# Beacon attention and a max-out FFN on one core: the first batch in token halves, loads reordered behind it

## The chip, the cores and the metric

The kernel runs on one core of a Trainium2 chip. The metric is the device time of one execution in microseconds; each time given for a kernel is a median of several executions. The profile is of one further execution and counts from its first instruction to its last (its span).

## The reference

Eight batches (B), eight heads (H), 576 tokens (S), head width 64 (D), 16 beacon keys and values ahead of the tokens. What is computed, cut to the core:

```
k_all, v_all = concat([beacon_k, k]), concat([beacon_v, v])      # 592 keys
scores = q @ k_all.T / 8 ; beacons seen by all, tokens causal
x = softmax(scores) @ v_all            -> (4608 tokens, 512)
h = max(x @ w1, x @ w2, x @ w3)        # 512 -> 768
out = h @ w_out                        # 768 -> 512, float32
```

Inputs and output are float32; the kernel multiplies in bf16.

## The kernel before

**Work.** Heads go in pairs: 4 pairs a batch, 32 pairs in all, and two pairs (a quad) share one product with the values. For a pair `p` the kernel loads q and k, casts them to bf16 (`cast_pair`, on POOL, L192), turns them so that the head width lies on the partitions (`turn`, `turn_apart`, `turn_pair`: transposes on TensorE, copies out of PSUM by DVE or ACT), and from batch 4 on has the DMA turn them by way of a copy in DRAM. `emit_scores` (L375) writes the transposed scores of one of four key-tile groups into a PSUM tile `sc` (two of them) and lets ACT exponentiate it into `at_sb`. `emit_masks` (L400) zeroes what lies past the diagonal, on POOL (an affine select, L410) or, for the first pairs, on DVE (a product with a triangle, L408). `emit_pv` (L430) makes, for one half of the tokens of a quad, the sums of the exponentials (weights of ones) and the products with the values; `finish_pv` (L462) inverts the sums on ACT (Ln, then Exp) and multiplies on DVE into `xT`, the FFN's input.

**FFN units.** Nine blocks of 512 tokens, each with 18 units `mm1_unit` (one weight matrix, 128 of 768 columns: 4 matmuls of 512 columns, then a copy or a running maximum on DVE) and 4 units `mm2_unit` (6 matmuls, a copy, a store). They stand in one list; `emit_ffn` (L543) takes the next one if a limit `allowed` permits and if the batches that it needs are finished (`ready`). They are what TensorE does between the pieces of attention.

**Order.** The program order on each engine is written out by hand. `start` and the table `fine_at` (L641) order pairs 0 to 4 in four steps a pair, with dummy matmuls (`keep_busy`) between them; later pairs have two steps (score groups 0 and 1; groups 2 and 3), and from pair 5 on `allowed` spreads 20 units over nine steps and then 22 units over each batch. The table `plan` hangs loads and casts on steps.

**Loads.** SP's queue carries q, k, v and the beacons, in the order of the list `loads` (L567); a cast through `C` (L580) is followed by the next load. Staging buffers `st`: 9. The FFN's weights are loaded and cast by POOL's own DMA queue (`load_w` L235, `load_w_out` L242): w1 at pair 2, w2 at the end of pair 3, w3 at pair 5, `w_out` at pair 6. POOL issues these in program order with its casts and masks. The values come in two pieces a batch (three and two key tiles), with one 256-byte run per token and head.

Of the kernel before, what the change touches and what calls it, by code (L numbers as in the profile page):

```python
# [16 lines left out]
def kernel(  # L17
# [29 lines left out]
    QR = 6  # L47
    QP = S // QR
    PR = 9
    PP = S // PR  # L50
    P_NINE = 4
# [18 lines left out]
    groups = [  # L70
# [5 lines left out]
    NG = len(groups)  # L76
    g_width = [sum(q1 - q0 for _, q0, q1 in pieces) for pieces in groups]
    g_base = [2 * sum(g_width[:gi]) for gi in range(NG)]
    AT_W = 2 * sum(g_width)
    assert max(g_width) <= 512  # L80
# [9 lines left out]
    st_pool = ctx.enter_context(tc.tile_pool(name="st", bufs=9))  # L90
    pair_pool = ctx.enter_context(tc.tile_pool(name="pair", bufs=3))
    v_pool = ctx.enter_context(tc.tile_pool(name="v", bufs=2))
# [25 lines left out]
    make_identity(nc, ident)  # L118
# [7 lines left out]
    for i in range(NT):  # L126
        z = const.tile([128, NKP], BF16, name=f"kT{i}")
        nc.vector.memset(z[:, NK:NKP], 0.0)
        kTs.append(z)
    nc.vector.memset(ones, 1.0)  # L130
    tri = const.tile([128, 128], BF16, name="tri")
    nc.gpsimd.memset(tri, 1.0)
    nc.gpsimd.affine_select(
        out=tri,
        in_=tri,
        compare_op=ALU.is_ge,
        fill=0.0,
        base=0,
        pattern=[[1, 128]],
        channel_multiplier=-1,  # L140
    )
# [19 lines left out]
    def load_pair(p, k_queue=None):  # L161
        b, g, j0 = place(p)
        hs = slice(head(g, j0), head(g, j0) + 2)
        st = new_stage(("pair", p))
        for i, (src, queue) in enumerate(((q, nc.sync), (k, k_queue or nc.sync))):
            if p < P_NINE:
                queue.dma_start(
                    out=st[:, i * PR * D : (i + 1) * PR * D],
                    in_=src[b, hs].rearrange("h (p r) d -> (h p) (r d)", r=PR),
                )  # L170
            else:
                queue.dma_start(  # L172
                    out=st[0:QP, i * NQ2 : (i + 1) * NQ2].rearrange("p (h x) -> p h x", h=2),
                    in_=src[b, hs].rearrange("h (p r) d -> p h (r d)", r=QR),
                )

    def cast_piece(p, i, cast):
        st = stage["pair", p]
        if p < P_NINE:
            t16 = pair_pool.tile([128, PR, D], BF16, name=f"t16{i}")  # L180
            cast(
                t16.rearrange("x r d -> x (r d)"), st[:, i * PR * D : (i + 1) * PR * D]
            )
        else:
            t16 = pair_pool.tile([QP, QR, 2, D], BF16, name=f"p16{i}")
            cast(  # L186
                t16.rearrange("p r h d -> p h r d"),
                st[0:QP, i * NQ2 : (i + 1) * NQ2].rearrange("p (h r d) -> p h r d", h=2, r=QR),
            )
        stage["pair16", p, i] = t16  # L190
# [26 lines left out]
    def cast_v(b, piece, cast):  # L217
# [6 lines left out]
        while t < t_hi:  # L224
            t1 = t + 1
            while b > 0 and t1 < t_hi and k_rows[t1] == k_rows[t]:
                t1 += 1
            n = k_rows[t]
            cast(  # L229
                v_sb[0:n, t:t1].rearrange("p t h d -> p (t h d)"),  # L230
                st[0:n, (t - t_lo) * H * D : (t1 - t_lo) * H * D],
            )
            t = t1

# [19 lines left out]
    def turn_beacons(b0, b1, src):  # L254
        n = Nb * (b1 - b0)
        ps = ffn_psum.tile([128, PPB, n], BF16, name="fps")
# [40 lines left out]
    def turn(p, i, ps):  # L297
        src = stage.pop(("pair16", p, i))
        if p >= P_NINE:
            for r in range(QR):  # L300
                nc.tensor.transpose(
                    ps[:, r * QP : (r + 1) * QP],
                    src[:, r].rearrange("p h d -> p (h d)"),
                    ident[0:QP, 0:QP],
                )
            return
        for r in range(PR):
            for e in range(2):
                hs = slice(64 * e, 64 * e + 64)
                nc.tensor.transpose(  # L310
                    ps[hs, r * PP : (r + 1) * PP],
                    src[hs, r],
                    ident[hs, hs],
                    tile_position=(64 * e, 64 * e),
                )

    def rows(p):
        return PR if p < P_NINE else QR

    def evac_q(p, ps, copy):  # L320
        copy(
            qTs[p % NT].rearrange("d (p r) -> d p r", r=rows(p)),
            ps.rearrange("d (r p) -> d p r", r=rows(p)),
        )
# [5 lines left out]
    def evac_k(p, ps, copy):  # L330
        kT = kTs[p % NT]
        copy(  # L332
            kT[:, Nb:NK].rearrange("d (p r) -> d p r", r=rows(p)),
            ps.rearrange("d (r p) -> d p r", r=rows(p)),
# [9 lines left out]
    def turn_pair(p, q_copy):  # L344
        banks = [pv_bank(i, [128, 1024], BF16) for i in range(2)]
        for i in range(2):
            turn(p, i, banks[i][:, 0:S])
        evac_q(p, banks[0][:, 0:S], q_copy)
        evac_k(p, banks[1][:, 0:S], by_dve)
# [12 lines left out]
    def at_view(p, t, e, q0, q1):  # L362
        for gi, pieces in enumerate(groups):
            off = g_base[gi] + e * g_width[gi]
            for t_, lo, hi in pieces:
                if t_ == t and lo <= q0 and q1 <= hi:
                    return at[p][0 : k_rows[t], off + q0 - lo : off + q1 - lo]
# [3 lines left out]
    def both_heads(p, gi):  # L371
        W = g_width[gi]
        return at[p][:, g_base[gi] : g_base[gi] + 2 * W].rearrange("k (e c) -> k e c", e=2)

    def emit_scores(p, gi):  # L375
# [6 lines left out]
        for t, q0, q1 in groups[gi]:  # L382
# [12 lines left out]
            out=both_heads(p, gi), in_=ps[:, :, 0 : g_width[gi]], func=AF.Exp, scale=scale  # L395
        )

    def emit_masks(p, gi, dve=False):
        off = 0
        for t, q0, q1 in groups[gi]:  # L400
            n = k_rows[t]
# [28 lines left out]
    def emit_pv(quad, hf, first=0, last=len(passes), apart=False):  # L430
        b, g = divmod(quad, n_quad)
        v_sb = v_tiles[b]
        if first == 0:
# [6 lines left out]
        for part, bank, lo, ca, cb in passes[first:last]:  # L440
            qa, qb = hf * HALF + ca, hf * HALF + cb
            ts = [t for t in range(n_kt) if q_min[t] < qb]
            for t in ts:
                q0 = max(qa, q_min[t])
                for j in range(4):
                    lhsT = (
                        ones[0 : k_rows[t]]
                        if part == 0
                        else v_sb[0 : k_rows[t], t, head(g, j), part - 1 : D : 2]
# [12 lines left out]
    def finish_pv():  # L462
# [3 lines left out]
        b, g = divmod(quad, n_quad)  # L466
# [5 lines left out]
        c0 = b % RING * S + hf * HALF  # L472
        for part, bank, lo, ca, cb in passes[1:]:
# [5 lines left out]
        if g == n_quad - 1 and hf == 1:  # L479
            ready[0] = b  # L480
# [3 lines left out]
    hTs = {}  # L484

    alone = [False]

    def mm1_unit(tb, ft, i, pool, name):
        if ft == 0 and i == 0:
            hTs[tb] = ffn_h.tile([128, n_ft, TOKB], BF16, name="hT")  # L490
        hT = hTs[tb]
# [12 lines left out]
        if i == 0:  # L504
            (by_act if alone[0] else by_dve)(hT[:, ft, :], ps)  # L505
        else:
            nc.vector.tensor_max(hT[:, ft, :], hT[:, ft, :], ps)  # L507
# [23 lines left out]

    units = []
    for tb in range(n_tokb):
        last_b = (TOKB * (tb + 1) - 1) // S
        for i in range(3):
            for ft in range(n_ft):
                units.append((last_b, mm1_unit, (tb, ft, i)))
        for tt in range(TOKB // 128):
            units.append((last_b, mm2_unit, (tb, tt)))
    UPB = len(units) // n_tokb  # L540
    done = [0]

    def emit_ffn(limit, pool=None, name="fps"):  # L543
        if done[0] + 1 <= limit and done[0] < len(units) and units[done[0]][0] <= ready[0]:
            _, fn, args = units[done[0]]
# [21 lines left out]
    loads = [L(load_pair, 0, nc.scalar), L(load_pair, 1, nc.scalar)] + load_pairs(2, 4)  # L567
    loads += [L(load_v, 0, 0), L(load_beacons, 1, B_PE, bk32_1), L(load_v, 0, 1)]
    loads += load_pairs(4, 7) + load_v_pieces(1) + load_pairs(7, 8)
# [17 lines left out]
    def start():  # L587
        keep_busy(15)
        next_load()
        load_beacons(0, 1, bk32_0, nc.scalar)  # L590
        next_load(10)
        cast_piece(0, 0, by_dve)
        cast_piece(0, 1, by_act)
        stage.pop(("pair", 0))
        by_pool(bk16_0, bk32_0)
        next_load()
        q_ps = ffn_psum.tile([128, S], BF16, name="fps")
        k_ps = ffn_psum.tile([128, S], BF16, name="fps")
        turn(0, 0, q_ps)
        turn(0, 1, k_ps)  # L600
        evac_q(0, q_ps, by_act)
        evac_k(0, k_ps, by_dve)
        turn_beacons(0, 1, bk16_0)
        keep_busy(4)
        C(cast_pair, 1, by_pool, by_pool)()
# [5 lines left out]


    P_FINE = PPB + 1

    def steps(p):
        return [[gi] for gi in range(NG)] if p < P_FINE else [[0, 1], [2, 3]]

    at_step(0, 0, C(cast_pair, 2, by_pool, by_pool))
    at_step(0, 1, C(cast_pair, 3, by_pool, by_pool))
    at_step(1, 0, *[L(emit_masks, 0, gi) for gi in range(NG)])  # L620
    at_step(1, 0, C(cast_v, 0, 0, by_pool))
    at_step(1, 1, C(cast_v, 0, 1, by_pool))
    at_step(1, 2, L(by_pool, bk16_1, bk32_1))
    at_step(1, 3, C(cast_pair, 4, by_pool, by_pool))
    at_step(2, 0, L(load_w, 0, 0, d_ff))
    at_step(2, 2, C(cast_pair, 5, by_pool, by_pool))
    at_step(3, 2, C(cast_pair, 6, by_pool, by_pool))
    at_step(3, 3, L(load_w, 1, 0, d_ff))
    at_step(4, 1, C(cast_v, 1, 0, by_pool))
    at_step(4, 2, C(cast_v, 1, 1, by_pool))  # L630
    at_step(5, 0, L(load_w, 2, 0, d_ff))
    at_step(5, 0, C(cast_pair, 7, by_pool, by_pool))
# [126 lines left out]
```

The softmax here doesn't subtract the row's maximum and nothing guards it: scores larger than these inputs give would overflow.

## Time and profile before

| | |
|---|---|
| median of 5 runs | 303.93 us (301.91 to 304.79) |
| profiled execution | 304.35 us |
| its span | 302.6 us |
| TensorE busy | 283.9 us, 94% of the span |
| DVE, ACT, POOL busy | 175.4, 143.2, 128.6 us |
| granted TensorE clock, mean | 0.982 |
| read from HBM, written | 35.13 MB, 14.22 MB |

In the profile a line such as `L497 PE MATMUL fps<-xT,w_sb` is a group of instructions of one source line; PE is TensorE, PEld its weight loads, DVE is VectorE, ACT ScalarE, POOL GpSimd, SPq the queue of SyncE that only issues DMAs. "Idle before" is time in which the engine did nothing ahead of an instruction, and the name behind the arrow is what ended it. In the tables of windows, PEclk is the granted TensorE clock (1.00 is full speed) and the DMA share is the mean busy share of 16 DMA engines; a mean above 1 comes from packets that overlap on an engine.

### The profile page before, as it was taken

What the parts mean: (1) busy time and instruction counts of PE and PEld (TensorE: products, weight loads), DVE (VectorE), ACT (ScalarE), POOL (GpSimd) and SP (SyncE); (2) the same over time, 40 slices, a digit from 0 to 9 for tenths busy, and PEclk for the clock granted to TensorE, in tenths of its full rate; (3) what the DMA queues carried; (4) which work ended last, traced back from release to release, by engine and by line L of the source; (5) the groups of instructions that cost most, each with busy time, mean ns of one, the idle gap of its engine ahead of it and who ended that gap; (6) DMA issues with size and microseconds to landing.
All of it is one profiled execution on the core that took longest, in us unless ns stands there. A gap on an engine that the chain in (4) does not pass through costs nothing.

```text
span 302.6 us, 8591 instructions
## 1 busy us (share of the span) xinstructions
PE 283.9 (94%) x3532; PEld 148.0 (49%) x3563; DVE 175.4 (58%) x330; ACT 143.2 (47%) x220; POOL 128.6 (42%) x261
## 2 busy tenths in 40 slices
PE   7796869999999999999999999999999999999995
PEld 4454234554455545454545687645454544444442
DVE  2968335656667466646564657365746575275373
ACT  3786554574555364635463556455545531400300
POOL 3876194455667684465446644562243210000000
PEclk9979797999999999999999999999999999999999
DMA  7999999999799889989998998466402001102003
GB/s 259 208 246 216 214 261 232 215 241 219 174 315 203 220 251 247 192 202 264 281 187 197 258 260 144 114 171 154 101 36 106 2 2 69 72 0 110 30 2 139
DMA packets 83095, 51.55 MB, mean 170 GB/s; under 512 B 62064, under 2 KB 76656, under 8 KB 83056
## 3 DMA queue, kind: packets, MB, share of 16 engines
q1 hardware_dynamic: 80976, 47.23, 66.8%
q0 software_dynamic: 1648, 3.15, 5.5%
q8 instruction: 28, 0.46, 0.7%
q10 hardware_dynamic: 432, 0.62, 0.7%
q14 instruction: 11, 0.09, 0.1%
HBM read 35.13 MB, written 14.22 MB: 163 GB/s over the span
## 4 chain that ended last, share of the span: by engine, by line
PE 80%; DMA 9%; SPq 3%; DVE 3%; POOL 2%; issue 2%; ACT 0%; DVEq 0%
PE fps L497 40%; PE fps L514 13%; PE pv L451 11%; PE sc L385 8%; PE sc L497 5%; DMA st<-in_v_dram 4%; DMA st<-in_k_dram 3%; PE sc L514 2%; DMA st<-in_q_dram 2%; SPq L249 1%; SPq L213 1%; POOL p L186 1%; DVE kT L332 1%; DVE hT L507 1%; SPq L172 1%
## 5 line engine op out<-in xcount | busy, mean ns | idle before, releaser
L394 ACT ACTIVATE at_sb<-sc 128x992 bf16<-128x992 f32 (+3 forms) x128 | 103.6, 862 | 100.8 <-PE sc L385 100.8
L497 PE MATMUL fps<-xT,w_sb 128*128 128x512 bf16 (+1 forms) x627 | 139.8, 360 | 3.1 <-issue 1.2
L497 PEld LDWEIGHTS <-w_sb 128*128 128x128 bf16 x720 | 66.1, 98 | 72.7 <-issue 17.3
L410 POOL TENSOR_SCALAR_AFFINE_SELECT at_sb<-at_sb 128x256 bf16<-128x256 bf16 (+2 forms) x145 | 52.7, 384 | 99.2 <-ACT at_sb L394 97.7
L507 DVE TENSOR_TENSOR hT<-hT,fps 128x512 bf16<-128x512 bf16 x96 | 65.8, 686 | 45.2 <-PE fps L497 45.1
L186 POOL CAST p<-st 96x768 bf16<-96x768 f32 x56 | 44.7, 823 | 1.6 <-DMA st<-in_q_dram 0.9
L514 PE MATMUL fps<-w_out_sb,hT 128*128 128x512 bf16 x173 | 40.6, 379 | 0.9 <-issue 0.8
L505 DVE CAST hT<-fps 128x512 bf16<-128x512 f32 x42 | 29.0, 690 | 21.5 <-PE fps L497 21.4
L385 PE MATMUL sc<-qT,kT 64*128 64x288 bf16 (+4 forms) x384 | 36.4, 288 | 3.0 <-ACT at_sb L394 1.2
L522 DVE COPY y<-fps 128x512 f32<-128x512 f32 x30 | 20.7, 689 | 27.9 <-PE fps L514 27.3
L514 PEld LDWEIGHTS <-hT 128*128 128x128 bf16 x216 | 20.5, 98 | 25.0 <-DVE hT L507 1.3
L474 DVE TENSOR_TENSOR xT<-pv,recip 128x288 bf16<-128x288 f32 (+2 forms) x93 | 27.2, 348 | 3.8 <-ACT recip L471 2.2
L451 PE MATMUL pv<-at_sb,v_sb 128*32 128x192 bf16 (+4 forms) x1352 | 28.6, 230 | 0.1
L385 PEld LDWEIGHTS <-kT 64*128 64x128 bf16 x384 | 13.8, 94 | 28.9 <-issue 19.8
L451 PEld LDWEIGHTS <-v_sb 128*32 128x32 bf16 (+1 forms) x1408 | 24.6, 97 | 3.3 <-issue 2.1
L229 POOL CAST v_sb<-st 128x512 bf16<-128x512 f32 (+2 forms) x26 | 21.5, 841 | 10.4 <-DMA st<-in_v_dram 10.3
L451 PE MATMUL pv<-at_sb,ones 128*32 128x288 bf16 (+4 forms) x492 | 17.6, 258 | 2.2 <-POOL at_sb L410 2.1
L497 PE MATMUL sc<-xT,w_sb 128*128 128x512 bf16 x71 | 18.3, 379 | 0.1
L469 ACT ACTIVATE lnd<-pv 128x288 f32<-128x288 f32 x31 | 12.9, 416 | 7.8 <-PE pv L451 7.8
L451 PEld LDWEIGHTS <-ones 128*32 128x32 bf16 (+1 forms) x512 | 11.0, 96 | 9.5 <-issue 7.8
L507 DVE TENSOR_TENSOR hT<-hT,sc 128x512 bf16<-128x512 bf16 x12 | 8.2, 688 | 12.5 <-PE sc L497 6.8
L505 ACT CAST hT<-sc 128x512 bf16<-128x512 f32 x6 | 3.5, 585 | 23.7 <-PE sc L497 23.7
(47 smaller groups left out, 115.5 us busy)
## 6 DMA issues: line engine op xcount, KB each, us to landing
st<-in_q_dram SPq DMA_DIRECT2D x32, 288.0 KB, 5.1
out_dram<-y SPq DMA_DIRECT2D x36, 256.0 KB, 2.4
st<-in_k_dram SPq DMA_DIRECT2D x30, 288.0 KB, 5.5
st<-in_v_dram SPq DMA_DIRECT2D x24, 256.0 KB, 6.1
w_sb<-in_moe_w_dram POOLq DMA_DIRECT2D x6, 384.0 KB, 9.4
q_dram<-p SPq DMA_DIRECT2D x16, 144.0 KB, 2.4
k_dram<-p SPq DMA_DIRECT2D x16, 144.0 KB, 2.4
st<-in_v_dram SPq DMA_DIRECT2D x8, 224.0 KB, 6.0
```

The lines of the kernel that those rows point to most:

```text
L186: cast(t16.rearrange("p r h d -> p h r d"), st[0:QP, i * NQ2 : (i + 1) * NQ2].rearrange("p (h r d) -> p h r d", h=2, r=QR),)
L229: cast(v_sb[0:n, t:t1].rearrange("p t h d -> p (t h d)"), st[0:n, (t - t_lo) * H * D : (t1 - t_lo) * H * D],)
L385: nc.tensor.matmul(ps[:, e, off : off + q1 - q0], kT[hs, 128 * t : 128 * t + 128], qT[hs, q0:q1], start=True, stop=True, tile_position=(64 ...
L394: nc.scalar.activation(out=both_heads(p, gi), in_=ps[:, :, 0 : g_width[gi]], func=AF.Exp, scale=scale)
L410: nc.gpsimd.affine_select(out=view, in_=view, compare_op=ALU.is_ge, fill=0.0, base=x0, pattern=[[0, 2], [1, hi - lo]], channel_multiplier=-1,)
L451: nc.tensor.matmul(ps[bank][32 * j : 32 * j + 32, lo + q0 - qa : lo + qb - qa], lhsT, at_view(PPQ * quad + j // 2, t, j % 2, q0, qb), star ...
L474: nc.vector.tensor_mul(xT[:, 2 * g + part - 1, c0 + ca : c0 + cb], ps[bank][:, lo : lo + cb - ca], recip[:, ca:cb],)
L497: nc.tensor.matmul(ps[:, o0 : o0 + n], w_in[i][:, ct, 128 * ft : 128 * (ft + 1)], xT[:, ct, x0 : x0 + n], start=(ct == 0), stop=(ct == n_c ...
L505: (by_act if alone[0] else by_dve)(hT[:, ft, :], ps)
L507: nc.vector.tensor_max(hT[:, ft, :], hT[:, ft, :], ps)
L514: nc.tensor.matmul(ps, hT[:, ft, 128 * tt : 128 * (tt + 1)], w_out_sb[:, ft, :], start=(ft == 0), stop=(ft == n_ft - 1),)
L522: nc.vector.tensor_copy(y, ps)
```

## The change

It rewrites the first batch and what feeds it, and moves some work in the later pairs. Lines here are of the file before unless the diff is meant.

- **Batch 0 in token halves.** q and k of pairs 0 to 3 are loaded as halves of 288 tokens on 96 partitions. The first halves of pairs 0 and 1 come by SP and ACT and are cast by DVE and ACT. All others come as six POOL transfers (`load_quad`: four heads of q or k, cast by the DMA), issued before anything else on POOL but two small masks. The score groups of batch 0 are cut so that group 0 holds all that the first 288 queries need; masks of the first halves go to DVE. A hand-written list `first_steps` replaces `fine_at`: group 0 of pairs 0 to 3 first, turns two pairs ahead, then the other groups. Eight dummy matmuls of the middle go, 12 + 2 instead of 15 + 4 stay at the start.
- **Loads.** Values of batch 0 come right behind the first two halves on SP. w1 is requested behind the cast of the third value tile, w2 behind that of the fifth, w3 behind the cast of pair 4, `w_out` in pair 5. The loads of pairs 4 and 5 wait for a one-column DVE memset of their buffer, which stands late in the first steps; all later SP loads stand behind them. Eight `st` buffers instead of nine.
- **First FFN block in halves.** Its units for w1 and w2 become 12 units of 256 tokens and two column tiles each (8 matmuls of 256 columns); the first six need only the first token halves. Six run within the first steps, the other 16 of the block are spread over 11 steps from pair 4 on.
- **Later pairs.** The turn of the next pair moves from the second step to the first and from the `pv` banks to an `sc` tile (pairs 7 to 15); its k is copied out before its q; the beacons' columns are copied by DVE instead of POOL. ACT inverts the sums right behind `emit_pv`, DVE multiplies at the end of the step. Some units use an `sc` tile.

```diff
+    groups_0 = [
+        [(0, 0, HALF), (1, q_min[1], HALF), (2, q_min[2], HALF)],
+        [(0, HALF, S), (3, q_min[3], S)],
+        [(1, HALF, S), (4, q_min[4], S)],
+        [(2, HALF, S)],
+    ]
...
+        if gate:
+            gate.memset(st[0:QP, 0:1], 0.0)
...
+    def load_quad(g, h):
+        for i in range(2):
+            t16 = const.tile([QP, 4, HR, D], BF16, name=f"quad{g}{h}{i}")
+            nc.gpsimd.dma_start(
+                out=t16.rearrange("p h r d -> p h (r d)"), in_=half_source(g, h, i, 0, 4)
+            )
...
-    def turn_pair(p, q_copy):
-        banks = [pv_bank(i, [128, 1024], BF16) for i in range(2)]
+    def turn_pair(p, q_copy, shared=True):
+        if shared:
+            ps = sc_psum.tile([128, 2, 1024], BF16, name="sc")
+            banks = [ps[:, i, 0:S] for i in range(2)]
...
-    loads = [L(load_pair, 0, nc.scalar), L(load_pair, 1, nc.scalar)] + load_pairs(2, 4)
-    loads += [L(load_v, 0, 0), L(load_beacons, 1, B_PE, bk32_1), L(load_v, 0, 1)]
-    loads += load_pairs(4, 7) + load_v_pieces(1) + load_pairs(7, 8)
+    loads = [L(load_v, 0, 0), L(load_v, 0, 1), L(load_beacons, 1, B_PE, bk32_1)]
+    loads += load_pairs(6, 7) + load_v_pieces(1) + load_pairs(7, 8)
...
+        load_quad(1, 0)
+        load_quad(0, 1)
+        load_quad(1, 1)
+        next_load(3)
...
+    first_steps = [
+        ((0, 0), [T(2, 0, False)]),
+        ((1, 0), [M(0, 0, True), T(3, 0, True), V(0), V(1)]),
+        ((2, 0), [T(0, 1, False), V(2), L(load_w, 0, 0, d_ff)]),
+        ((3, 0), [T(1, 1, True), M(1, 0, True), M(2, 0, True)]),
+        ((0, 1), [M(0, 1)]),
+        ((0, 2), [T(2, 1, False), M(3, 0, True), M(0, 2), V(3), V(4)]),
+        ((0, 3), [M(0, 3, True), L(load_w, 1, 0, d_ff)]),
+        ((1, 1), [P(0, 0), M(1, 1)]),
+        ((1, 2), [T(3, 1, False), finish_pv, M(1, 2)]),
+        ((1, 3), [P(1, 0, True), M(1, 3, True)]),
+        ((2, 1), [finish_pv, G(4), cast_p]),
+        ((2, 2), [M(2, 1), M(2, 2, True)]),
+        ((2, 3), [P(0, 1, False, 0, 2), F(1), M(2, 3)]),
+        ((3, 1), [P(0, 1, False, 2, 4), M(3, 1, True), G(5), F(1), L(turn_beacons, 1, B_PE, bk16_1)]),
+        ((3, 2), [F(1), finish_pv, next_7, M(3, 2)]),
+        ((3, 3), [F(2), M(3, 3), L(cast_pair, 4, by_pool, by_pool), L(load_w, 2, 0, d_ff), P(1, 1),
+                  L(turn_apart, 4, 0), L(turn_apart, 4, 1), finish_pv, F(1), L(cast_pair, 5, by_pool, by_pool)]),
+    ]
+    at_step(4, 0, C(cast_pair, 6, by_pool, by_pool))
+    at_step(5, 0, C(cast_v, 1, 0, by_pool))
+    at_step(5, 0, L(load_w_out))
+    at_step(5, 1, C(cast_v, 1, 1, by_pool))
+    at_step(5, 1, C(cast_pair, 7, by_pool, by_pool))
...
+        if tb == 0:
+            for n, lo in ((0, 0), (need, MID)):
+                for i in range(2):
+                    for ft in range(0, n_ft, 2):
+                        units.append((n, mm1_halves, (tb, ft, i, lo, lo + MID)))
...
-                    if n_step <= 9:
-                        allowed = 2 + n_step * (UPB - 2) / 9
+                if n_step <= N_FIRST:
+                    allowed = first + n_step * (UPB - first) / N_FIRST
```

In `first_steps`, T turns a half, M masks, P is `emit_pv`, V casts a value tile, G is a gated pair load and F runs FFN units. `N_FIRST` is 11, and `first` is 6.

## The prediction

> **What bounds the kernel now.** I read the busy time by stage first, because the page's totals (TensorE 94%) mix stages. Columns: busy us and count for PE, PEld, DVE, ACT, POOL, then granted clock, DMA share, GB/s. I cut where pair 4's scores, pair 5's, pair 9's and the tail begin.
>
> ```profile
> 0.00:25.00 25.00, 19.47 (x359) 11.33 (x359) 15.91 (x36) 17.18 (x26) 15.88 (x33) 0.93 0.99 235
> 25.00:35.40 10.40, 7.76 (x151) 4.08 (x152) 5.35 (x16) 4.86 (x9) 2.90 (x6) 0.85 1.14 222
> 35.40:66.30 30.90, 27.04 (x330) 13.09 (x334) 16.69 (x30) 17.64 (x26) 18.60 (x40) 0.94 1.10 232
> 66.30:250.00 183.70, 181.20 (x2433) 97.33 (x2458) 110.68 (x209) 95.65 (x146) 91.20 (x183) 1.00 0.78 180
> 250.00:302.60 52.60, 48.46 (x271) 22.13 (x268) 26.73 (x41) 7.87 (x14) 0.00 (x0) 0.99 0.16 61
> ```
>
> From 66.3 us on TensorE is the bound, with 2.5 us idle in 184; only more work or new stalls count there. Before 66.3 no engine is full, the clock sags, and the DMA share is 1. The chain of waits, followed back from 60 us, says that the DMA orders this stage:
>
> ```profile
> 16.46 8.76 DMA st<-in_k_dram
> 25.28 0.83 POOL p L186
> ...
> 26.22 13.05 DMA st<-in_v_dram
> 39.32 0.61 POOL v_sb L229
> ...
> 42.42 1.59 POOL p L186 x2
> 44.01 0.72 POOL at_sb L410 x2
> 44.77 0.65 PE pv L451 x33
> ```
>
> Batch 1's last values take from 26.2 to 39.3 us; then POOL casts pair 7 before it masks what TensorE waits for. TensorE's timeline shows what such waits cost twice:
>
> ```profile
> 32.75 2.76 PE L497 MATMUL fps<-xT,w_sb 128*128 128x512 bf16 x6 [0.22 <-issue]
> ...
> 44.42 0.55 PE L451 MATMUL pv<-at_sb,ones 128*32 128x176 bf16 x6 [2.11 <-POOL at_sb L410]
> ...
> 45.58 2.87 PE L497 MATMUL fps<-xT,w_sb 128*128 128x512 bf16 x7 [0.16 <-issue]
> ```
>
> Behind a lull, matmuls stand 0.43 us apart; unhindered ones 0.216. The value loads are late because of who shares the DMA (queues, 26 to 34 us, then 38 to 46 us: packets, MB, share of 16 engines):
>
> ```profile
> q0 software_dynamic: 513, 1.43, 90.6%
> q1 hardware_dynamic: 1134, 0.29, 19.3%
> ```
> ```profile
> q1 hardware_dynamic: 1476, 2.09, 108.5%
> ```
>
> Weights (POOL's queue) take the engines; 256-byte value packets get little.
>
> **What the skill says.** "DMA: Bandwidth & Descriptors", section Queues, rings and completion order: an engine takes queues in turn, a packet each; so weights win time by packet size. The 90.6 against 19.3% agree. "TensorE: Matmul & The Clock Gate", Part 1: idle TensorE falls to half its clock, in windows of 3413 ns; the trace's 0.43 against 0.216 us agrees. "GPSIMD Engine Reference", section Key points: POOL shares its SBUF interfaces with DVE instructions that have two SBUF inputs or use a two-port mode. The same beacon copy agrees (min/median/max ns):
>
> ```profile
> L328 POOL COPY kT<-bT x10: 186/193/194, 41.2 to 111.2; 128x16 bf16<-128x16 bf16 x10
> L328 DVE COPY kT<-bT x5: 155/550/2166, 9.5 to 27.7; 128x16 bf16<-128x16 bf16 x5
> ```
>
> **Where to compare.** Before, 19 FFN units are done when pair 9's scores start (66.3 us); after the change 6+16x10/11 = 20. The extra one is an `mm2` unit, 6x0.216 = 1.3 us. So the mark to beat is 67.6 us. From there both run the same units (22 by the next step, 22 a batch).
>
> **The DMA sum.** Prices: an `mm1` weight 4.0 us (q0: 0.906x8 us for 1.43 MB written; one weight is 0.79 MB); a pair of 0.59 MB on 96 partitions 2.25 us (2.09 MB in 8 us); a batch of values, 1.18 MB in 256-byte packets, 5.8 us (the queues of 57.8 to 60.3 us give 204 GB/s); the four beacon loads about 0.6. First packets move at 2 us. No row shows the six quad transfers (1.77 MB read in 768-byte runs, written as 384 bytes). Below: 5.2 us at `w_out`'s read rate (queues of 52 to 57 us: 0.70 MB written, twice that read, in 0.819x5 us, 342 GB/s). Above: 13.5, if they go at half the 96-partition rate. I take that rate, 262 GB/s: 6.8.
>
> After, in the order of need: start 2.0, first halves 2.25, quads 6.8, values 5.8, beacons 0.6 = 17.4. Then w1 and w2 8.0, pairs 4 to 6 6.8, w3 4.0, batch 1's values 5.8, pair 7 2.25 = 44.3. `w_out` is requested when three tiles of batch 1's values are cast (about 43) and takes turns with pair 7: +2. Lane waits idle the DMA a little (before: share 0.64 in 12 to 15 us, 1.1 lost): +1. Pair 7 lands at about 47. Before it landed at about 41, but w3 and `w_out` only afterwards, and three of its first pairs went at 400 GB/s on 128 partitions.
>
> **TensorE from pair 7 on.** The changed order turns pair 7 in pair 6's first step, and TensorE is in order: all behind it waits. POOL casts its k (0.82): 47.8; 12 transposes 0.5: 48.3. Rest of pair 6: two units of 4x0.216 = 0.86, scores 0.5, gaps 0.2: 50.5. Pair 7: scores 1.06, products 1.61, turn 0.5, three units 2.6, gaps 0.2 = 6.0: 56.5. Pair 8: 1.06+0.79+0.5+0.86+two `mm2` 2.6+0.2 = 6.0: 62.5. Pairs 8 and 9 land 2.25 us apart behind pair 7 plus the rest of `w_out`, ahead of their turns at about 53 and 59. **Gain 67.6-62.5 = 5.1 us.**
>
> **Is TensorE there by then?** First steps, per engine: ACT 16 exponentials 13, inversions 4x0.85, small ones 1.5 = 17.9; DVE 16 half copies of 0.40 (half of 0.75), masks 3.5, FFN copies 6x0.69, xT 4x0.88, casts and pair 4's copies 3.5 = 21. From 4.2 us on that is 25 at least. The values come 1:1 with quad packets, so their third tile lands near 16; its cast frees w1's request (before at 20.7) and the first value products. The fifth tile then shares with w1, so w2 is asked for near 21. That pushes my walk along TensorE's order to pair 4's scores at about 34. Pairs 4 and 5 (4 us each: scores 1.06, turn 0.5, 2 to 3 units) end at 42: ahead of pair 7's 47. So the first steps have 4 us of cover; beyond that they cost one for one. The gates cost nothing: they hold pair 4 back to about 23, while w1 and w2 fill the engines; pair 4 then lands near 29, its cast ends by 31.
>
> **The rest.** Eight dummy matmuls (0.33 each) go: they filled waits, so nothing; cover gone, a half-clock window of 3.4 us costs up to 1.7. Before had three by 66.3 us; I expect as many (0, range -1.7 to +1.7). The turn a step earlier, k first: turned batches take 32.8 and 31.6 us against 30.5 unturned; 12 transposes a pair explain 2.0 and 1.5, so at most 0.3 in the one, nothing in the other. An `sc` tile taken by a turn makes group 3 wait for q's copy (ACT 0.65), hidden by a unit. Beacon copies on DVE: 0.15 if POOL is quiet, 2.17 at worst; DVE is 60% busy and TensorE has two `fps` banks (1.7 us) ahead, so 0 to 0.5 each for 11 pairs. Later inversion order, DVE products at the step's end, `sc` for units: the batches without turns show 0.2 us idle in 30.5, so nothing to win. I take 0 for all.
>
> 302.6-5.1 = 297.5 of span; with the 1.7 us around it 299.3. The profiled execution is 0.4 above the median: 298.9, say **299**.
>
> **Rivals.**
> A, the above: the DMA paces pairs 5 to 7, gain 3 to 7. Chance 0.50; 297 to 301.
> B, TensorE-bound refill: if weights overlap better with value packets (shares add up to 1.1), pair 7 is on time and TensorE runs through: 34 + 12 `mm1` 10.4 + two `mm2` 2.6 + five pairs at 3.0 less two value products 2.4 = 59.6, gain 8: 296, down to 293. Against it: before, the same engines were full up to 66 us. Chance 0.20.
> C, it does not do what it says: the weights' requests sit behind value casts on POOL in order, so they come no sooner; `w_out` ahead of pair 7 and a cold clock use up the rest. Gain 0 to 2: 302 to 304. Chance 0.13.
> D, slower: the quads. All turns of six of eight halves hang on them. At 13.5 us instead of 6.8 everything behind, the weights too, is 7 us late: 306. From 8 us more (15 us; over 100 ns for each of the 144 packets an engine) it is slower than 307. For it: small written packets, POOL's descriptor queue beside busy DVE; against: 1024-byte packets of `w_out` do well. With the beacon copies stalling as well, 308. Chance 0.17.
>
> **Numbers.** Likeliest A, 299, its own range 296 to 302. Leaving out D and the edge of B gives 293 to 306. About 1% (3 us) is what a measurement of this kernel tells from no change. Faster than 300.9: A 0.42, B 0.20, C 0.03 = 0.65; within: A 0.08, C 0.10 = 0.18; slower 0.17.
>
> **What would show it.** Right: quads landed by 15 to 16 us; pair 4's scores at 31 to 35; the chain before 60 us still DMA into POOL casts; TensorE waiting at pair 7's transposes till about 48; pair 9's scores at about 62; batches from pair 9 on 30.5 to 32.8 as before. Wrong: first turns waiting for quads beyond 18 us; DVE's beacon copies near 2 us in pairs 6 to 15; batches longer by 0.5 us.

## The result, and the profile after

The change brought nothing: 304.38 us median (302.69 to 308.42, 41 runs) against 303.25 (301.48 to 306.08, 78 runs), ratio 1.0043, 95% interval 1.003 to 1.0057, so slower by some 0.4%. Forecast was 299. Ratios here leave out single slow executions and come near the ratio of the means, so they differ from the ratio of the listed medians by up to 0.002. The profiled execution took 303.93 us, its span 302.2; the one before had 304.35 and 302.6. Profiles of single executions thus differ by 1.5 us from what the medians say, and nothing below rests on less than that unless several profiles agree.

Times by stage, columns as before, cut at pair 4's, pair 9's scores and the tail (first line: up to 25 us):

```profile
0.00:25.00 25.00, 20.20 (x280) 11.09 (x284) 12.30 (x51) 14.10 (x22) 12.61 (x29) 0.65 1.02 174
25.00:37.20 12.20, 11.61 (x214) 8.25 (x207) 6.71 (x18) 4.76 (x10) 5.13 (x9) 0.87 0.76 177
37.20:66.60 29.40, 25.88 (x368) 15.16 (x372) 18.31 (x36) 21.23 (x31) 18.03 (x37) 1.00 1.14 235
66.60:250.00 183.40, 180.53 (x2475) 97.62 (x2498) 113.43 (x214) 96.60 (x147) 91.60 (x179) 1.00 0.87 186
250.00:302.20 52.20, 47.35 (x215) 21.24 (x218) 26.20 (x40) 7.57 (x14) 0.00 (x0) 0.99 0.16 61
```

Pair 4's scores come at 37.2 us (before 25), pair 9's at 66.5, where the forecast had 62.5 and the mark to beat was 67.6. So 1.1 us was won by then. Behind it the step from pair 12's first exponential to pair 13's is 0.4 us longer (8.51 against 8.13) and the stretch behind pair 31 0.6 longer; 0.3 is won between. What is new is in the first two rows: a clock of 0.65 in the first, a DMA share of 0.76 between 25 and 37 us, and fewer GB/s in both. SP's waits between 15 and 47 us name the reason (total, times, longest):

```profile
SPq L180 <- DVE at_sb L468: 9.6, 1, 9.6
SPq L180 <- DVE st L178: 3.4, 1, 3.4
```

L178 is the gate's memset, L468 a mask that stands ahead of the other one on DVE. SP, with all later loads in its queue, stood 13 us at two one-column memsets. The chain of waits, followed back from 60 us, goes through them:

```profile
29.79 0.31 SPq L180
...
33.69 11.40 DMA st<-in_v_dram
...
45.24 1.46 POOL v_sb L261
46.70 0.79 POOL w_out_sb L288
47.51 0.77 POOL at_sb L470 x2
48.28 0.60 POOL v_sb L261 x2
...
50.10 0.83 POOL p L218
...
50.98 0.44 PE sc L345 x6
```

Read it upwards from pair 7's turn on TensorE (50.98): it waits for POOL's cast of pair 7; POOL is in order and still has values, masks and `w_out`'s request ahead of it; those waited for one value tile, 256 KB, that took 11.4 us; that tile was issued late because of the gate of pair 5 at 29.79. While it is under way it meets w3, requested at 34.4 (queues between 34 and 44 us: packets, MB, share of 16 engines):

```profile
q1 hardware_dynamic: 4273, 1.40, 76.0%
q0 software_dynamic: 288, 0.79, 40.5%
```

TensorE's timeline shows what that costs, and a second wait, for the beacon copy that moved to DVE:

```profile
42.05 0.54 PE L442 MATMUL sc<-qT,kT 64*128 64x288 bf16 x8 [1.18 <-DVE kT L380]
...
50.20 0.43 PE L345 MATMUL sc<-ident,p 96*128 96x96 bf16 x6 [0.24 <-POOL p L218]
50.98 0.43 PE L345 MATMUL sc<-ident,p 96*128 96x96 bf16 x6 [0.35 <-POOL p L218]
```

The beacon copy as a group (min/median/max ns), one of them twelve times the median:

```profile
L380 DVE COPY kT<-bT x15: 153/161/1897, 8.1 to 111.2; 128x16 bf16<-128x16 bf16 x15
```

### The profile page after: what moved, and what is told of

It reads as the page before. It is cut to its first block, busy times and chain, and to the rows that moved or that the text cites. A ratio compares the mean times of both kernels' runs of the same rounds, so it can differ in the third digit from the quotient of the medians.

```text
span 302.2 us, 8581 instructions
## 1 busy us (share of the span) xinstructions
PE 285.6 (94%) x3536; PEld 153.4 (51%) x3566; DVE 177.0 (59%) x357; ACT 144.3 (48%) x221; POOL 127.4 (42%) x253
## 4 chain that ended last, share of the span: by engine, by line
PE 81%; DMA 6%; POOL 3%; DVE 3%; ACT 2%; issue 2%; SPq 1%; POOLq 0%; DVEq 0%
PE fps L574 30%; PE sc L574 12%; PE pv L514 12%; PE fps L610 11%; PE sc L442 8%; PE sc L610 4%; DMA st<-in_v_dram 4%; DMA quad<-in_k_dram 3%; ACT at_sb L451 2%; PE sc L345 1%; DVE y L618 1%; SPq L180 1%; POOL quad L209 1%; POOL v_sb L261 1%; PE fps L514 1%
## 5 line engine op out<-in xcount | busy, mean ns | idle before, releaser
L451 ACT ACTIVATE at_sb<-sc 128x928 bf16<-128x928 f32 (+5 forms) x128 | 103.9, 861 | 90.1 <-PE sc L442 89.0
L574 PE MATMUL fps<-xT,w_sb 128*128 128x512 bf16 (+1 forms) x464 | 106.4, 356 | 2.4 <-issue 0.8
L584 DVE TENSOR_TENSOR hT<-hT,fps 128x512 bf16<-128x512 bf16 x70 | 47.9, 687 | 29.3 <-PE fps L574 28.7
L574 PE MATMUL sc<-xT,w_sb 128*128 128x512 bf16 (+1 forms) x187 | 42.9, 356 | 0.1
L442 PE MATMUL sc<-qT,kT 64*128 64x288 bf16 (+5 forms) x400 | 38.1, 292 | 3.0 <-ACT at_sb L451 1.5
L610 PE MATMUL fps<-w_out_sb,hT 128*128 128x512 bf16 x149 | 36.1, 379 | 0.9 <-issue 0.6
L584 DVE TENSOR_TENSOR hT<-hT,sc 128x512 bf16<-128x512 bf16 x32 | 22.0, 687 | 16.4 <-PE sc L574 10.6
L514 PE MATMUL pv<-at_sb,v_sb 128*32 128x288 bf16 (+5 forms) x1376 | 29.6, 232 | 0.0
L582 DVE CAST hT<-fps 128x512 bf16<-128x512 f32 x32 | 22.0, 690 | 12.1 <-PE fps L574 12.1
L261 POOL CAST v_sb<-st 128x1536 bf16<-128x1536 f32 (+2 forms) x21 | 18.4, 893 | 0.6 <-DMA st<-in_v_dram 0.6
L514 PEld LDWEIGHTS <-ones 128*32 128x32 bf16 (+2 forms) x512 | 11.2, 97 | 8.7 <-issue 7.0
```

The source lines that it names most:

```text
L261: cast(v_sb[0:n, t:t1].rearrange("p t h d -> p (t h d)"), st[0:n, (t - t_lo) * H * D : (t1 - t_lo) * H * D],)
L442: nc.tensor.matmul(ps[:, e, off : off + q1 - q0], kT[hs, 128 * t : 128 * t + 128], qT[hs, q0:q1], start=True, stop=True, tile_position=(64 ...
L451: nc.scalar.activation(out=both_heads(p, gi), in_=ps[:, :, 0 : g_width(p, gi)], func=AF.Exp, scale=scale)
L514: nc.tensor.matmul(ps[bank][32 * j : 32 * j + 32, lo + q0 - qa : lo + qb - qa], lhsT, at_view(PPQ * quad + j // 2, t, j % 2, q0, qb), star ...
L574: nc.tensor.matmul(ps[:, o0 : o0 + n], w_in[i][:, ct, 128 * ft : 128 * (ft + 1)], xT[:, ct, x0 : x0 + n], start=(ct == 0), stop=(ct == n_c ...
L582: (by_act if alone[0] else by_dve)(h, ps)
```

## Experiments

In the tables "pair n" is the start of pair n's first exponential in the profiled execution, "4 to 5" the step from pair 4's to pair 5's. A profile is one execution, and single ones differ: kernels that run the same up to pair 13 (after and e0; g2) took 8.51, 9.82 and 8.40 us from pair 12 to 13. Every ratio is to the kernel before, on the same chip.

**Gates and clock.** In the profile after, TensorE ran at half clock from 7.7 to 28.1 us. Theory at this point: the gate and this clock take 3 to 4 us each.

e0_after_again: the kernel after, unchanged. 

> The changed kernel once more, beside the others on one chip, and for a second trace. Both theories: about 1.004 of the time before (1.003 to 1.006). Theory 'gates' (the pair loads held back by the memset leave the DMA idle, and pair 7 and batch 1's values come late): pair 7 lands near 50 us again and pair 9's scores start near 66 us even if TensorE's clock happens to be full in the first steps. Theory 'cold clock' (TensorE at half clock from 8 to 28 us lengthens the first steps): if the clock is full this time, pair 4's scores start 4 us or more before 37 us and the end moves with it.

e1_no_gate:
```diff
-        return L(load_pair, p, nc.vector)
+        return L(load_pair, p)
```


> Pairs 4 and 5 are loaded without the DVE memset; all else as changed. Theory 'gates': SP's loads go out from about 16 us, DMA share stays near 1 from 24 to 33 us, pair 7 lands at 43 to 45 us instead of 50, pair 9's scores start at 62.5 to 63.5 instead of 66.5 us: 3 to 4 us less than the changed kernel, about 0.99 of before. Theory 'cold clock': the first steps still end at 37 us; at most 1 us gained.

e2_warm: dummy matmuls into the `sc` tile ahead of the score groups of the first steps (31 by the table in the code, and three more at the start).
```diff
+        for _ in range(warm.get((p, gi), 0)):
+            nc.tensor.matmul(
+                ps[:, 0, 0:320], busy[:, 0:128], busy[:, 0:320], start=True, stop=True
+            )
...
-        keep_busy(2)
+        keep_busy(5)
```


> 32 dummy matmuls of 320 columns stand in front of the score groups of the first steps (and three more at the start), to keep TensorE's clock up; gates as changed. Theory 'cold clock': full clock from 5 us on, pair 4's scores at 31 to 33 us instead of 37, gates open 3 to 4 us earlier, pair 9's scores at 62 to 63.5: 3 to 4 us less than the changed kernel. Theory 'gates': clock full, first steps perhaps shorter by 1 to 3 us, but the end within 1 us except by what the gates open earlier.

e3_warm_no_gate: both. 

> Both edits. If the two costs stand in different places: 6 to 7 us less than the changed kernel, about 0.98 of before, pair 9's scores at 59.5 to 60.5. If only the gates count: as without gates. If only the clock counts: as with the dummies.

| | median us | ratio (95%) | pair 4 | pair 7 | pair 9 | span |
|---|---|---|---|---|---|---|
| before | 303.56 | | 25.4 | 52.2 | 66.7 | 302.6 |
| e0 after | 304.57 | 1.003 (1.001 to 1.0049) | 37.9 | 54.5 | 66.9 | 303.3 |
| e1 no gate | 302.95 | 0.9987 (0.9969 to 1.0005) | 38.5 | 54.9 | 67.3 | 301.7 |
| e2 warm | 303.23 | 1.0006 (0.9982 to 1.0029) | 36.1 | 54.8 | 67.1 | 303.2 |
| e3 both | 301.63 | 0.994 (0.9917 to 0.9963) | 35.9 | 52.2 | 64.6 | 299.0 |

Against e0, in the medians e1 brings 1.6 us, e2 1.3 and both 2.9 (by the ratios 1.3, 0.7 and 2.7), less than half of what was expected. In the profiles e1's pair 7 is no earlier than e0's; up to pair 13 it gains only in the step from pair 12 to 13 (8.13 us). e2's pair 7 can't be compared: its first exponential came at 10.2 us against 7.9 in e0, since the five dummies at its start still ran at half speed (1.51 us; 0.85 in e3, whose first exponential came at 8.2). The profiles of e4, e5, g0, g1 and h2 began as late, at 9.9 to 10.1. That e3 moves pair 7 by 2.3 us and e1 does not fits two chains that meet there, the loads and TensorE's own work, of which the later counts.

The clock is a cost of its own, and the mean granted clock of an execution doesn't show it. The record of the clock in a trace begins at its first change, and the time ahead of that counts as full: in every trace the first dummies stand 0.267 us apart, while full clock in e3 makes that 0.14. In g3, h1 and h4 below, three kernels without added dummies, the record begins only at 27.4 to 29.9 us and the mean reads 0.998 to 1.000. Yet twelve transposes take 0.69 us in them at 13 us, as in the kernel after with its mean of 0.964 (first line), and not 0.45 as in e3 (second):

```profile
13.07 0.69 PE L360 MATMUL pv<-ident,quad 96*64 96x96 bf16 x12
```
```profile
13.06 0.45 PE L360 MATMUL pv<-ident,quad 96*64 96x96 bf16 x12
```

So all eight profiles of kernels without added dummies (after, e0, e1, g2, g3, h1, h3, h4) run at half clock from 9 to 27 us, whatever their mean. Executions can't be sorted into cold and warm ones by it; what the clock costs is read from the dummies.

**Queues.** On top of e3:

e4_pool_beacons:
```diff
-                        place_beacons(p + 1, by_dve)
+                        place_beacons(p + 1, by_pool)
```


> Base: the kernel with ungated loads and warm first steps (span 299.0, pair 9's scores at 64.6). One edit: from pair 5 on the beacons' columns are copied by POOL instead of DVE. In the base DVE's copy for pair 5 took 2.12 us and TensorE waited 1.39 us for it. Queue theory (waits in in-order queues, not the DMA, hold pairs 4 to 9 back): the step from pair 4 to pair 5 falls from 4.9 to about 3.5 us and the span by 1.0 to 1.4. Rival, the DMA paces this stage: the 1.4 us comes back as a longer wait for pair 7's cast, span down by 0.3 or less. Second rival: on POOL the copy stands behind the pair cast and a mask, so TensorE waits as long as before, change 0.

e5_pair7_first:
```diff
-    loads += load_pairs(6, 7) + load_v_pieces(1) + load_pairs(7, 8)
+    loads += load_pairs(6, 7) + [L(load_v, 1, 0)] + load_pairs(7, 8) + [L(load_v, 1, 1)]
...
-    at_step(5, 1, C(cast_v, 1, 1, by_pool))
     at_step(5, 1, C(cast_pair, 7, by_pool, by_pool))
+    at_step(5, 1, C(cast_v, 1, 1, by_pool))
```


> Same base. One edit: pair 7 is loaded, and cast on POOL, ahead of the second piece of batch 1's values, which nothing needs before pair 7's step. In the base pair 7 landed at 45.1 and its cast ended at 48.5, and TensorE waited twice for it, 0.25 and 0.34 us, with units put between. Queue theory: pair 7 lands near 43, its cast starts behind the first value cast and two masks at about 45.9, 1.0 to 1.2 earlier; the wait of 0.6 goes, and the step from pair 6 to 7 falls from 7.2 to about 6.5; span down by 0.5 to 0.7. Rival: POOL's order only swaps who waits; the value cast behind it delays the products of pair 7's step, change 0 within 0.3.

e6_early4: `cast_pair(4)` behind the turn of the beacons, its two `turn_apart` behind the unit of (3, 2) and ahead of those of (3, 3). 

> Same base. One edit: pair 4, landed at about 25 without the gate, is cast on POOL before the last masks of batch 0 instead of behind them, and is turned between the FFN units of the last two groups instead of behind the last products. In the base the end of batch 0 is a chain (exponential, mask, two casts 1.6 us, turn 0.7, copies 1.5) with ACT idle 2.8 and 1.9 us. Queue theory: pair 4's scores come at about 34.2 instead of 35.9, and the gain of 1.5 is kept to the end, span near 297.5. Rival, the DMA paces: pair 4 starts earlier but pair 7 still lands at 45, so pair 7's first exponential stays within 0.5 of 52.2 and the span within 0.5 of 299.

e7_all: the three together. 

> The three edits together on the same base. Queue theory: gains add, 3 to 3.5 us: pair 9's scores at about 61.3, span 295.5 to 296, time near 298. Rival, the DMA paces: span 298 or more, TensorE waiting over 2 us for pairs 7 to 9 in place of the waits taken out.

| | median us | ratio (95%) | pair 4 | 4 to 5 | 6 to 7 | pair 9 | 12 to 13 | span |
|---|---|---|---|---|---|---|---|---|
| e3 (again) | 301.63 | 0.994 (0.9917 to 0.9963) | 35.9 | 4.92 | 7.17 | 64.6 | 8.13 | 299.0 |
| e4 | 300.18 | 0.9896 (0.9855 to 0.9938) | 36.4 | 3.67 | 6.91 | 64.0 | 8.45 | 298.7 |
| e5 | 301.07 | 0.9931 (0.9906 to 0.9955) | 38.5 | 4.91 | 6.30 | 66.3 | 8.13 | 300.8 |
| e6 | 301.31 | 0.9938 (0.9909 to 0.9968) | 36.0 | 4.91 | 7.15 | 64.7 | 8.13 | 299.1 |
| e7 | 299.97 | 0.9896 (0.9851 to 0.9941) | 36.2 | 3.68 | 6.05 | 63.0 | 9.30 | 298.6 |

The beacon copy did what was expected in its step (4.92 to 3.67), and so did pair 7 first (7.17 to 6.30; in this profile the first exponential came 1.9 us later than in e3 and pair 4's 2.6 later, so its span says nothing). e6 fell through: the turns of pair 4 went in earlier and units waited for DVE's copies in their place (0.30, 0.25 and 0.42 us on TensorE), so pair 4 came when it had come before. Together pair 9 comes at 63.0, 1.6 earlier than in e3, but three pairs later 1.2 us is lost again. The place is POOL; in the kernel after, too, it stood 3.74 us there:

```profile
86.67 0.61 POOL L665 CAST bk<-bk 64x512 bf16<-64x512 f32 x1 [3.74 <-DMA bk<-in_beacon_k_dram]
```

This casts the beacon keys of batches 4 to 8; pair 11's masks and a pair cast stand behind it. In the kernel before these keys landed at 79.9 us and nothing waited for them.

**The beacon keys earlier.** In the next eight kernels (g and h) pairs 16 to 31 come from DRAM by a plain copy instead of one that transposes, so batches 4 to 8 of their output are not the reference's. No such fetch is issued ahead of pair 13, so that up to there they run as their counterparts above.

g0_all_plain: e7 so. 

> A new base: the kernel with all edits so far, except that pairs 16 to 31 are fetched from DRAM as they lie, by a plain copy, and not turned: batches 4 to 8 of its output are not the reference's. The first such fetch is issued when pair 13 starts, so up to there it should be the kernel before it: pair 9's scores at 63.0 from a first exponential at 8.2, the step from pair 12 to 13 at 9.3 us with POOL waiting for the last beacon keys. The span may differ by a few us either way behind pair 16.

g1_all_bk_plain:
```diff
-        if b == B_PE:
-            loads.append(L(load_beacons, B_PE, B, bk32))
-        loads += load_pairs(b * PPB, (b + 1) * PPB) + load_v_pieces(b)
+        loads += load_pairs(b * PPB, (b + 1) * PPB)
+        if b == B_PE - 1:
+            loads.append(L(load_beacons, B_PE, B, bk32))
+        loads += load_v_pieces(b)
```


> That base (pairs 16 to 31 not turned) with one edit: the beacon keys of batches 4 to 8 are loaded ahead of batch 3's values instead of behind them. In the base they landed at 83.5, POOL stood 4.71 us waiting to cast them, with pair 11's masks behind, and the step from pair 12 to 13 took 9.30 us instead of 8.13. Queue theory: the step falls back to about 8.1 and the time by about 1.2. Rival, the DMA is late there as a whole: values or pair 13 come late instead, the step stays at 9.0 or more and the time within 0.4 of the base's.

g2_after_plain: the kernel after so. 

> The kernel after the change, except that pairs 16 to 31 are fetched as they lie and not turned (batches 4 to 8 are not the reference's): the base for the next run. Up to pair 13 as the kernel after: the step from pair 12 to 13 at 8.5 to 9.8 us, POOL waiting 3.7 to 4.5 us for the beacon keys.

g3_after_bk_plain: g2 with g1's edit. 

> The kernel of the run before this one with the beacon keys of batches 4 to 8 ahead of batch 3's values. Queue theory: the step from pair 12 to 13 falls to about 8.1 and the time by 0.4 to 1.7 us. Rival: there is slack for it elsewhere, time within 0.3 of its base.

| | median us | ratio (95%) | pair 9 | 12 to 13 | pair 13 |
|---|---|---|---|---|---|
| g0 | 300.36 | 0.9893 (0.9846 to 0.994) | 64.5 | 8.13 | 95.9 |
| g1 | 300.35 | 0.9896 (0.986 to 0.9931) | 63.3 | 10.23 | 96.8 |
| g2 | 304.18 | 1.0016 (0.9992 to 1.004) | 67.4 | 8.40 | 99.1 |
| g3 | 304.77 | 1.0027 (1.0003 to 1.0051) | 67.2 | 8.40 | 98.9 |

The rival holds: neither g1 nor g3 is faster than its base. In g1 POOL no longer waits for the beacon keys but for the next thing in the queue, pair 16, whose q landed at 86.1 (POOL had stood 5.03 us by then) and k at 87.1; masks of pair 12 stand behind it and TensorE waits for them (POOL, then TensorE):

```profile
87.29 0.82 POOL L218 CAST p<-st 96x768 bf16<-96x768 f32 x1 [0.26 <-DMA st<-in_k_dram]
88.07 0.76 POOL L483 TENSOR_SCALAR_AFFINE_SELECT at_sb<-at_sb 128x256 bf16<-128x256 bf16 x2
```
```profile
88.52 0.56 PE L527 MATMUL pv<-at_sb,ones 128*32 128x176 bf16 x6 [1.57 <-POOL at_sb L483]
```

So the loads as a whole are late there, not one of them. In e3, e4, e7, g0 and g1 pair 9 lies between 63.0 and 64.6, yet pair 13 between 95.6 and 96.8: the earlier pair 9, the more the step from pair 12 to 13 takes (8.13 us at 64.5 and 64.6, 8.45 at 64.0, 9.30 and 10.23 at 63.0 and 63.3). In the kernel before pair 16's k landed at 85.1, 6.3 us ahead of pair 12's first exponential; in the kernel after at 88.8, 1.5 ahead; in g0 at 85.2, 2.6 ahead. Without gates the stream is where it was, and TensorE has caught up with it. e7 and g0 show it best: the same kernel up to pair 13, g0's pair 9 is 1.5 us later after a late start, and its pair 13 only 0.4. The order is not strict in other kernels: h1 below has pair 9 at 64.9 and 8.84 us for that step.

**How much each, with the others out.**

h1_no_gate_queues: g2 without gates, with the edits of e4 and e5, no dummies added. 

> The kernel after (pairs 16 to 31 fetched unturned, so batches 4 to 8 are not the reference's; base 304.18) with ungated loads, the beacons' columns by POOL, and pair 7 ahead of the second value piece; no dummies added, first steps otherwise as they were. If the slow clock costs time of its own, this is 1 to 1.6 us slower than the kernel that has the dummies too (300.36): 301.4 to 302. If the clock is covered, since executions with full clock took as long as the others, it takes 300.4 within 0.5.

h2_all_gated: g0 with the gates back. 

> The kernel with all edits (pairs 16 to 31 unturned; base 300.36), with the memset gates of pairs 4 and 5 put back. Gate theory: everything later on SP waits, pair 7 lands near 48 and later pairs 3 to 4 us later than in the base, TensorE waits for pair 7's cast: 2 to 3.5 us slower, 302.4 to 303.8. Rival, the gate hurt only beside the slow clock: within 0.5 of the base.

h3_gated_queues: g2 with the edits of e4 and e5 only. 

> The kernel after (pairs 16 to 31 unturned; base 304.18) with only the two queue edits: beacons by POOL, and pair 7 ahead of the second value piece. Gates and clock as they were. If waits add, 1.3 to 2.2 us faster: 302 to 302.9. If pair 7's late landing behind the gate rules, TensorE waits for it all the same: within 0.6 of 304.2.

| dummies | queue edits | with gates | without gates |
|---|---|---|---|
| no | no | e0: 1.003 (1.001 to 1.0049); g2: 1.0016 (0.9992 to 1.004) | e1: 0.9987 (0.9969 to 1.0005) |
| yes | no | e2: 1.0006 (0.9982 to 1.0029) | e3: 0.994 (0.9917 to 0.9963) |
| no | yes | h3: 1.0046 (1.0025 to 1.0067) | h1: 0.9942 (0.9921 to 0.9963) |
| yes | yes | h2: 0.9978 (0.9955 to 1.0001) | g0: 0.9893 (0.9846 to 0.994) |

Times: h1 301.46, h2 302.9, h3 304.65. In the last row, g0 and h2, e6's edit is in as well; alone it changed nothing. Without the gate the queue edits bring 0.0045 to 0.0047, some 1.4 us. Behind it they bring nothing without dummies (h3, as the gate theory said) and 0.8 with them, which is within the uncertainty. The gate costs 1.3 us in the first row (0.9 if g2 is taken) and 2.0, 3.2 and 2.6 in the others (differences of the ratios by 303.5, each uncertain by about 1). The dummies bring 1.4 to 1.5 us without gates (e1 to e3, h1 to g0), as forecast for h1 in case the slow clock costs time of its own, and 0.7 and 2.1 with them (e0 to e2, h3 to h2). That "executions with full clock took as long as the others", as the expectation of h1 has it, rests on the mean clock and doesn't hold.

h4_w3_late: h3 with w3 requested later.
```diff
-        ((3, 3), [F(2), M(3, 3), L(cast_pair, 4, by_pool, by_pool), L(load_w, 2, 0, d_ff), P(1, 1),
+        ((3, 3), [F(2), M(3, 3), L(cast_pair, 4, by_pool, by_pool), P(1, 1),
...
+    at_step(4, 0, L(load_w, 2, 0, d_ff))
     at_step(4, 0, C(cast_pair, 6, by_pool, by_pool))
```


> The kernel with gates and the two queue edits (pairs 16 to 31 unturned, so batches 4 to 8 are not the reference's; 304.65), with w3 requested ahead of pair 6's cast, at about 40 us instead of 35. There the third value tile of batch 1 was issued at 33.9 and landed at 46.0, behind w3, POOL waited 2.07 us to cast it with masks behind, and the step from pair 6 to 7 took 9.5 us. Sharing theory: the tile lands near 40, the wait goes, that step falls to 6.1 to 7, and the time by 2 to 3 us, if w3 is there (about 48) for its first unit at about 50. Idle theory: what the gate held back is late anyway, the tile still lands after 44 and the time stays within 0.7.

Measured: 304.7, ratio 1.0052 (1.0028 to 1.0076). The wait went as sharing said. In h3 POOL waited for the tile (first line), masks stood behind, and TensorE waited for them (second fence):

```profile
46.13 1.46 POOL L261 CAST v_sb<-st 128x1536 bf16<-128x1536 f32 x1 [2.07 <-DMA st<-in_v_dram]
```
```profile
48.87 0.55 PE L519 MATMUL pv<-at_sb,ones 128*32 128x176 bf16 x6 [1.62 <-POOL at_sb L475]
```

In h4 the tile landed at 41.8 instead of 46.0 and POOL did not wait for it:

```profile
44.98 1.46 POOL L261 CAST v_sb<-st 128x1536 bf16<-128x1536 f32 x1
```

The step from pair 6 to 7 fell from 9.50 to 6.23 and pair 9 came at 66.7 instead of 68.4. But behind it the stream was hardly earlier than in h3 (pair 8's k at 53.6 against 54.5, pair 9's at 57.2 against 58.0), the step from pair 12 to 13 stayed at 9.85 (9.91), and the median did not move. Part of that fall belongs to h3's profile: it is the slowest of its 22 executions (306.33), with half clock from 49.6 to 53.0 us. So sharing with w3 makes that one tile 4.7 us slower (12.0 us from issue to landing against 7.4); that the time is set by how late the whole stream is fits the step from pair 12 to 13, and isn't shown by an experiment of its own.

## Why the prediction was wrong

The likeliest case was A, "the DMA paces pairs 5 to 7", with a gain of 5.1 us. Its chain is in the profile, DMA into POOL's cast into pair 7's turn, but two terms that it put at nothing were not nothing: the gates, the failed step, and the clock. With both out (e3) the kernel gains 2.7 us by the ratios, with the queue edits (e7) 4.1; that is 3.2 ahead of the kernel before, and the rest of the 5.1 did not come.

- **The gates (the failed step).** "The gates cost nothing: they hold pair 4 back to about 23, while w1 and w2 fill the engines." Pair 4 was issued at 25.4, pair 5 at 29.8. From 18 to 24 us the engines were indeed full (1.06 and 1.08); then w2 ran out, landing at 26.7, and until 29.8 only pair 4 was left to load (last two columns: DMA share, GB/s; three lines of the kernel after, then of e3):

```profile
24.00:27.00 3.00, 3.00 (x47) 2.01 (x46) 1.04 (x5) 1.62 (x3) 0.44 (x2) 0.50 0.70 153
27.00:30.00 3.00, 3.00 (x57) 1.83 (x57) 0.99 (x3) 1.00 (x1) 0.00 (x0) 0.81 0.50 153
30.00:33.00 3.00, 3.00 (x32) 2.29 (x33) 2.32 (x6) 2.29 (x5) 0.71 (x3) 1.00 0.66 178
```
```profile
24.00:27.00 3.00, 2.78 (x79) 1.87 (x66) 1.64 (x5) 1.88 (x3) 0.33 (x1) 1.00 1.08 243
27.00:30.00 3.00, 2.71 (x29) 1.61 (x27) 1.83 (x4) 2.17 (x6) 0.32 (x1) 1.00 1.07 273
30.00:33.00 3.00, 3.00 (x82) 2.55 (x86) 2.08 (x5) 0.33 (x1) 2.60 (x5) 1.00 1.23 225
```

  Idle shares of 0.30, 0.50 and 0.34 in these windows of 3 us make 3.4 us of lost transfer (an estimate, as shares can pass 1); the sum had 1 for all lulls. In e1, which differs by the gates alone, the three shares are 1.08, 1.07 and 1.19. (The lull from 15 to 18 us, 0.54, is there without gates too, 0.58 in e1.) I costed what the gated pair needs and forgot its queue: pairs 6 and 7, all values and, much later, pair 16 stand behind it on SP. Pair 7's k landed at 49.96 instead of 47, its turn ended at 51.4 instead of 48.3; with 15.1 instead of 14.2 us from there to pair 9's scores this is the whole gap of 4.0 us in the profile. The runs put the gates at 0.9 to 3.2 us, and they are only a part of the gap.
- **The cover.** "The first steps have 4 us of cover." Pair 4's scores came at 37.2 instead of 34. Inside the cover as I had worked it out, and yet e1, with pair 7 landed by 45.8, did not turn it earlier: from pair 4's first exponential to pair 7's TensorE took 14.4 us in e7, where nothing held it for long, and 16.4 in e1 with the waits for the beacon copy and for POOL's cast. With scores at 34 that makes pair 7's at 48.4 in place of the forecast's 50.5: about 2 us of cover, and under 1 with the beacon copy's 1.2. I had counted pairs 4 and 5 to their end and left out the half of pair 6 ahead of pair 7's turn. This fits that removing the gate alone does not move pair 7. (The sum behind the 50.5 leaves out its own 0.2 of gaps; that changes nothing.)
- **The clock.** I expected as many half-clock windows as before, three, and put them at 0. The record has 20.5 us of half clock in one piece, as long as six windows of the 3.4 us that I had counted with, and the first dummies stand half as fast as later ones even ahead of it. Keeping the clock up brings 0.7 to 2.1 us, 1.4 to 1.5 without gates. So the half clock is the second term that failed.
- **Beacon copies on DVE, "0 to 0.5 each".** One took 1.90 us, right behind POOL's pair cast, and TensorE had no units ahead: 1.2 us. In e4 the step is 1.25 shorter; the median copy took 0.16.
- **The later pairs, taken as 0.** True of their own work: from pair 9 to 12 and from pair 13 to 31, the sums are the same to 0.1 us in all profiles with the change, but for e2's, which took 1.3 us more from 9 to 12. Not true of the loads: I had 40 us of DMA sum and stopped at pair 9, though the DMA share stays near 1 (1.03 from 75 to 90 us in the kernel after, 1.20 from 90 to 105). The gain of 5.1 could not have been kept whole: at best, in e7, pair 13 came at 95.6, 4.0 us ahead of before, and the span was 298.6.
- **Rivals.** D fell: quads landed between 7.5 and 15.0 us, as forecast. B (TensorE runs through) is what e7 comes near to. C, at 302 to 304, comes nearest to what was measured: its reason, that the weights "come no sooner", is wrong (w1 was requested at 16.1, before at 20.7), its "does not do what it says" is right by way of the gate. What I had quoted from before, small value packets losing against a weight's, the change made anew with w3, and I did not look for it there.

Left open: the last stretch after pair 31 takes 65.0 us in the profiles of the kernel after, e0, e2 and g2, 64.6 to 64.7 in the other changed ones and 64.4 before; it was not followed up. No run has full clock in the first steps without dummies, so what they do besides is not separated. Nor is it settled where the rest of the 5.1 us went: the meeting with the load stream at pair 13 accounts for 1.2 us in e7.

A version that beats both kernels is e7: 299.97, ratio 0.9896 (0.9851 to 0.9941); e4, simpler by two edits, is not told apart from it.

## What to carry to other kernels

A wait put on one transfer is a wait for everything behind it in that queue: price it at the queue's last urgent entry, and check that the engines it frees have other work in every window of the hold. When DMA is full for the first third of a kernel, sum the stream to where its share falls below 1, not to the end of the stage that you change: time won early can be given back where the compute meets the stream. Before trusting a slack, walk both chains to the instruction where they meet. And a mean granted clock near 1 is no proof of full clock at the start: compare the spacing of equal matmuls.

## What the runs showed of the hardware

In the kernel after TensorE stood at half clock from 7.7 to 28.1 us, although it was busy for 2.2 to 3.0 us of each 3 us from 9 us on (first busy time: TensorE's; third figure from the end: clock):

```profile
12.00:15.00 3.00, 2.85 (x38) 1.73 (x38) 2.17 (x9) 2.16 (x3) 0.61 (x1) 0.50 1.28 213
15.00:18.00 3.00, 2.77 (x44) 1.10 (x44) 1.98 (x9) 2.54 (x4) 2.48 (x6) 0.50 0.54 97
18.00:21.00 3.00, 3.00 (x58) 1.54 (x58) 1.11 (x3) 1.85 (x4) 3.00 (x7) 0.50 1.06 201
```

Between 7 and 26 us its tiles had 64 rows or 32 columns, or were transposes of 96x96. In the eight profiles without added dummies full clock came 1.3 to 3.8 us after the first matmuls of 128x128 (2.0 in the kernel after). In those with dummies of 128x128 between such tiles, the clock rose at 5.2 to 16.1 us. The Trainium skill, "TensorE: Matmul & The Clock Gate", Part 1, has an activity monitor grant the clock; these traces show that for such tiles the busy time of the profile is not what it goes by. What it does count is not shown.

The same 4 KB copy on DVE took 0.16 us, or 1.50 (e6), 1.90 (after) and 2.12 (e3) when POOL's cast of a pair ran beside it. Each time it ended within 0.03 us of the end of POOL's unbroken work: in e6 of the cast (33.3), in the kernel after and in e3 of the masks behind the cast (42.0 and 40.2). The Trainium skill, "GPSIMD Engine Reference", section Key points, has GpSimd share its SBUF interfaces with VectorE and contend with instructions of VectorE in a two-port mode or with two SBUF inputs. That fits, though no run shows in which mode this copy runs; the size is this case's.
